# Six score banks filled by four row tiles at once, 256-query attention chunks, and an issue order that knows the array modes, in a two-layer attention and mixer kernel

## The chip, the cores and the metric

The kernel runs on one core of one Trainium2 chip. The metric is the device time of one execution in microseconds (us), taken on the slowest core, which here is the only one. The times of one kernel mostly agreed within 1% from run to run, so each number below is a median of several runs, and ratios have a 95% interval. For a program on one core the state of a single run cannot be told, but every profiled run of which several executions were timed was counted as fast. The span of a profiled execution is a little shorter than its device time. The kernel before was profiled in one more execution, of 591.3 us with a span of 589.2 us, which is not among the runs of its median.

The engines are named as in the profile: PE is TensorE (matrix multiply), PEld the weight loads of TensorE, DVE is VectorE, ACT is ScalarE, POOL is GpSimd and SP is the engine that issues the DMAs.

## The reference

The input `x` has 2048 tokens of 512 bf16 numbers. Two identical layers run on it. A layer is a causal attention with a sliding window of 256 tokens, 32 heads of 16 numbers each, and then an MLP that mixes over tokens.

```python
def _A_ref(x, wqkv, wo):
    B, S, D = x.shape                      # 1, 2048, 512
    H = 32; Dh = D // H; W = 256
    q, k, v = ...                          # x @ wqkv, cut into 32 heads of 16
    scores = jnp.einsum("bhqd,bhkd->bhqk", q, k) * (Dh ** -0.5)
    mask = (idx[:, None] - idx[None, :] >= 0) & (idx[:, None] - idx[None, :] < W)
    p = _softmax(jnp.where(mask[None, None], scores, -1e9))
    o = jnp.einsum("bhqk,bhkd->bhqd", p, v)
    return ...(o) @ wo

def _B_ref(x, w1, b1, w2, b2):             # w1: 2048 x 1792, w2: 1792 x 2048
    h = _layernorm(x, axis=-1)
    u = _gelu(jnp.einsum("bsd,sf->bdf", h, w1) + b1)
    y = jnp.einsum("bdf,fs->bds", u, w2) + b2
    return y.transpose(0, 2, 1)

x = x + _A_ref(_layernorm(x), wqkv, wo);  x = x + _B_ref(_layernorm(x), w1, b1, w2, b2)
x = x + _A_ref(_layernorm(x), wqkv, wo);  x = x + _B_ref(_layernorm(x), w1, b1, w2, b2)
```

## The kernel before

The kernel is written as a graph. Each operation says which engine it is for, what it reads and writes, a modelled cost and perhaps a priority. A list scheduler in the kernel's Python walks through the graph with the modelled costs and so fixes the order of instructions of every engine before the program runs. A `Pool` has a number of buffers; a `Tile` of a pool takes a buffer when its first operation is placed and gives it back after its last.

A head has only 16 numbers, so a head alone would use a small part of the 128x128 array of TensorE. The kernel takes the heads in four groups of eight ("octets", index `o`). Within an octet, two heads share a row tile of 32 partitions `r`. A score matmul reads 32 rows (`kbd`, keys of two heads in block diagonal form) and writes 128 partitions, so four of them, at the four row positions, can be in the array at once. The product of probabilities and values (PV, with `vbd`), and the sum of probabilities (the denominator, with `onesbd`), read 128 rows and write 32 partitions, so they use four column positions. All other matmuls use the whole array or halves of it. They are called fillers below: the projections to q, k and v, the output projection `wo`, the MLP.

PSUM has eight banks of 512 f32 columns. Before, they are given out as two score buffers of two banks (`psum2`), and four single banks (`psum`), of which fillers may hold two. A score operation computes two row tiles, over up to 512 columns, and ScalarE takes both in one exp instruction:

```python
psum2 = Pool("psum2", 2)
psum = Pool("psum", 4)
psum.classes = {"od": [0, 4], "f": [0, 2], "y": [0, 4]}
...
for u0 in range(0, len(lanes), 2):                    # two row tiles at a time
    ts = Tile(psum2)
    def f_sc(e, ts=ts, rr=prs[u0:u0 + 2], runs=runs, o=o):
        for j, q0, n, c0 in runs:
            tkk, jj = tk(j)
            for i, r in enumerate(rr):
                last = e.matmul(PS[:, 2 * ts.slot + i, c0 * 64:(c0 + n) * 64],
                                lhsT=kbd[32 * r:32 * r + 32, tkk.slot, o, jj, :, :]...,
                                rhs=qT[32 * r:32 * r + 32, tq.slot, o, q0 * 64:(q0 + n) * 64],
                                ..., tile_position=(32 * r, 0))
        return last
    prev_sc[0] = op("tensor", f_sc, ..., writes=[ts], prio=-1e6 + len(g.ops), ...)
    def f_exp(e, ...):
        return e.activation(pt[...], PS[:, 2 * ts.slot:2 * ts.slot + 2, 0:n], ACTF.Exp, scale=SMSCALE)
```

After a mask multiply on VectorE, PV and the denominator follow, in two separate banks `tO` and `tDen`, with 512 queries at a time. ScalarE computes one over the denominator as exp(-ln(d)), and VectorE multiplies. The scheduler picks by priority alone: scores, then PV, then fillers in program order. Fillers include a transpose of every token tile on TensorE, in `qkv`:

```python
def qkv(m):                                            # block m of 512 tokens
    for i in range(4):
        ft = filler()                                  # one of the two filler banks
        def f_tr(e, t=t, ft=ft):
            for c in range(4):
                last = e.transpose(PS[:, 4 + ft.slot, :]..., xh_sb[:, t, c * P:(c + 1) * P], ident[:])
        ...                                            # then a copy PSUM -> xhT on VectorE
...
for layer in range(2):
    prepare(0)                                         # layer 2: y of the first MLP, layernorm, qkv
    prepare(1)
    for m in range(4):
        tos[m] = attention(m, tqs[m], tks)             # 512 queries
        ...                                            # wo_block (4 tiles), prepare(m + 2)
    w1t = [load_w1(fb) for fb in range(7)]             # 1 MB each, two buffers w1b
    w2t = [load_w2(i) for i in range(8)]               # 0.9 MB each, two buffers w2b
    u_phase(w1t)                                       # u = gelu(w1^T h)
```

The second half of the MLP (`y_block`) of layer 1 is part of `prepare` in layer 2, so it runs as a filler between the scores of layer 2.

The softmax here doesn't subtract the row's maximum and nothing guards it: scores larger than these inputs give would overflow.

## Time and profile before

The time before was 593.02 us (three runs, 590.82 to 593.85). The span of the profiled execution is cut into five stages by the events on ScalarE: the first exp of layer 1, its last exp, the last gelu of layer 1, the first exp of layer 2 and its last exp.

| Stage | us | TensorE busy | ScalarE busy |
|---|---|---|---|
| start | 17.9 | | |
| attention of layer 1 (A1) | 172.3 | 155.8 | 155.6 |
| rest of the first MLP's u | 63.1 | 59.9 | 12.1 |
| gap without exp | 25.5 | 24.1 | 1.3 |
| attention of layer 2 (A2), with the rest of y of layer 1 | 194.2 | 180.1 | 156.7 |
| last MLP | 116.2 | 105.0 | 12.1 |

The table is read off the windows view of the kernel before, last five stages. Its columns are the window and its length in us, then busy us and, in brackets, the number of instructions of PE, PEld, DVE, ACT and POOL, then the granted TensorE clock as a share of full speed, the busy share of the DMA engines, and GB/s.

```profile
17.90:190.20 172.30, 155.77 (x2570) 73.17 (x2588) 118.00 (x245) 155.60 (x182) 68.80 (x109) 0.96 0.10 25
190.20:253.30 63.10, 59.91 (x290) 25.71 (x294) 7.73 (x18) 12.08 (x17) 3.04 (x8) 0.98 0.37 101
253.30:278.80 25.50, 24.07 (x166) 11.93 (x170) 18.03 (x37) 1.33 (x2) 10.31 (x22) 1.00 0.55 150
278.80:473.00 194.20, 180.11 (x2624) 80.19 (x2657) 125.57 (x245) 156.71 (x182) 61.45 (x99) 0.96 0.09 26
473.00:589.20 116.20, 105.04 (x486) 45.53 (x494) 18.91 (x34) 12.13 (x17) 3.04 (x8) 0.97 0.39 111
```

Two engines are 90% busy in A1, so neither alone is the limit at every moment. In A2 TensorE is 93% busy and ScalarE 81%. The next lines, from the page of the kernel before, are the busy sums of the engines, the granted TensorE clock in tenths for 40 equal slices of the span, and the groups of the exps and of the score matmuls. A group is line, engine, operation, output and inputs, shapes and count, then busy us and mean ns, then idle time of the engine ahead of them and what ended most of it.

```profile
PE 533.3 (91%) x6171; PEld 240.1 (41%) x6240; DVE 299.5 (51%) x610; ACT 339.1 (58%) x400; POOL 152.8 (26%) x266
PEclk9989999999995999999999999999999589999899
L600 ACT ACTIVATE pt<-PS 128x1024 bf16<-128x1024 f32 (+1 forms) x304 | 288.8, 1033 | 88.1 <-PE PS L587 71.4
L587 PE MATMUL PS<-qT,kbd 32*128 32x320 bf16 (+4 forms) x1440 | 120.9, 262 | 12.0 <-ACT pt L600 9.4
```

The exps cost 288.8 us in 304 instructions; ScalarE was idle 71.4 us in front of them because a score matmul had not been issued or was not done. The score matmuls kept TensorE busy for 120.9 us. The clock fell to half in two of the slices.

The next four lines, from the TensorE timeline of the kernel before (start us, busy us, instructions), show what a score operation costs between fillers.

```profile
104.17 0.39 PE L587 MATMUL PS<-qT,kbd 32*128 32x320 bf16 x4
104.49 0.60 PE L499 MATMUL PS<-xhT,wqkv 128*128 128x512 bf16 x2
105.03 0.39 PE L587 MATMUL PS<-qT,kbd 32*128 32x192 bf16 x4
105.36 0.60 PE L499 MATMUL PS<-xhT,wqkv 128*128 128x512 bf16 x2
```

Ends are modelled, so starts are what to compare. A score operation of 2 row tiles and 512 columns plus two full-array matmuls repeats every 0.86 us (104.17 to 105.03). Back to back, full-array matmuls of 512 columns follow each other every 0.216 us in most cases in this trace, so three passes of 512 columns (one for the score operation, two for the fillers) take 0.65 us. What remains, 0.21 us, is put down here to two changes of array mode, at about 0.11 us each. The Trainium skill says in "TensorEngine Tiling (Array Packing)", Key Properties, that "Changing tiling mode (not just tile) drains the TensorE", without a time.

The ScalarE timeline of the kernel before has one long hole in layer 2, and its chain of waits, in order of time (start us, us), goes through a weight load in each MLP.

```profile
379.49 2.85 ACT L600 ACTIVATE pt<-PS 128x1024 bf16<-128x1024 f32 x3 [20.53 <-PE PS L587]
```

```profile
207.99 6.07 DMA w1b<-in_B_w_dram
541.83 5.62 DMA w2b<-in_B_w_dram
```

The hole of 20.53 us ends with a score matmul: for that time TensorE worked on fillers, with no score operation ready to run.

### The profile page before, as it was taken

The page shows a single profiled execution, that of the slowest core. Times are in us where ns is not written, and L with a number is a line of the kernel's source. Part 1 is how long each engine was busy: PE and PEld are TensorE (multiplying, and loading weights), DVE is VectorE, ACT ScalarE, POOL GpSimd, SP SyncE. Part 2 cuts the span into 40 slices and gives each one's busy share as a digit, 9 for nine tenths or more (in the row PEclk, how much of TensorE's full clock was granted, in tenths as well). Part 3 has the DMA queues.
Part 4 walks back from the last instruction along what each step waited for, and adds up shares of the span by engine and source line. Part 5 has one row for each costly group of instructions (what it writes and reads, how often), then busy time and mean ns, then how long its engine had stood idle before and what let it go on. Part 6 is the DMA issues. An engine that isn't in the chain of part 4 may idle for free.

```text
span 589.2 us, 13839 instructions
## 1 busy us (share of the span) xinstructions
PE 533.3 (91%) x6171; PEld 240.1 (41%) x6240; DVE 299.5 (51%) x610; ACT 339.1 (58%) x400; POOL 152.8 (26%) x266
## 2 busy tenths in 40 slices
PE   4879999999988989989999999999998799997897
PEld 1435444444333434444344434434433343443343
DVE  5986665865873400056766466856687341001021
ACT  0678999699898121110998992299869821111000
POOL 3772433444320200015315212621453001000000
PEclk9989999999995999999999999999999589999899
DMA  8920000000000055572020022202000005251663
GB/s 276 225 54 3 3 1 2 3 2 2 1 2 2 1 143 142 143 197 63 2 63 3 2 59 69 63 3 61 5 2 3 1 1 142 71 143 28 186 187 117
DMA packets 68299, 36.55 MB, mean 62 GB/s; under 512 B 4752, under 2 KB 68240, under 8 KB 68240
## 3 DMA queue, kind: packets, MB, share of 16 engines
q1 hardware_dynamic: 68240, 35.66, 21.8%
q8 instruction: 49, 0.80, 0.6%
q14 instruction: 10, 0.08, 0.0%
HBM read 33.56 MB, written 2.10 MB: 61 GB/s over the span
## 4 chain that ended last, share of the span: by engine, by line
PE 57%; ACT 20%; DVE 14%; POOL 4%; DMA 3%; issue 2%; DVEq 0%; POOLq 0%
ACT pt L600 17%; PE PS L722 15%; PE PS L708 15%; PE PS L587 8%; PE PS L499 7%; PE PS L648 6%; DVE stats L438 4%; PE PS L524 4%; DVE x_sb L677 2%; POOL rstd L449 2%; PE PS L674 2%; DVE pt L621 2%; DVE xh_sb L451 2%; ACT rl L661 1%; ACT rl L663 1%
## 5 line engine op out<-in xcount | busy, mean ns | idle before, releaser
L600 ACT ACTIVATE pt<-PS 128x1024 bf16<-128x1024 f32 (+1 forms) x304 | 288.8, 1033 | 88.1 <-PE PS L587 71.4
L587 PE MATMUL PS<-qT,kbd 32*128 32x320 bf16 (+4 forms) x1440 | 120.9, 262 | 12.0 <-ACT pt L600 9.4
L722 PE MATMUL PS<-uT,w2b 128*128 128x512 bf16 x429 | 105.9, 385 | 10.8 <-DMA w2b<-in_B_w_dram 4.8
L708 PE MATMUL PS<-xh_sb,w1b 128*128 128x512 bf16 x436 | 101.0, 383 | 3.0 <-DVE xh_sb L451 1.0
L726 DVE SCALAR_TENSOR_TENSOR x_sb<-PS,b2col,x_sb 128x512 bf16<-128x512 f32 x32 | 22.9, 746 | 141.8 <-PE PS L722 141.8
L648 PE MATMUL PS<-pt,vbd 128*32 128x320 bf16 (+4 forms) x1440 | 86.4, 270 | 7.7 <-DVE pt L621 2.8
L621 DVE TENSOR_TENSOR pt<-pt,ldm 128x1024 bf16<-128x1024 bf16 (+2 forms) x104 | 65.8, 632 | 52.0 <-ACT pt L600 51.7
L648 PE MATMUL PS<-pt,onesbd 128*32 128x320 bf16 (+4 forms) x1440 | 82.7, 267 | 0.0
L587 PEld LDWEIGHTS PS<-qT,kbd 32*128 32x128 bf16 x1440 | 40.5, 94 | 99.6 <-ACT pt L600 58.1
L715 ACT ACTIVATE uT<-PS,b1col 128x512 bf16<-128x512 f32 x28 | 19.2, 687 | 98.2 <-PE PS L708 98.2
L499 PE MATMUL PS<-xhT,wqkv 128*128 128x512 bf16 x227 | 68.5, 393 | 6.1 <-issue 4.4
L447 POOL TENSOR_SCALAR rstd<-agg 128x1 f32<-128x1 f32 x64 | 16.1, 251 | 220.1 <-DVE agg L440 217.6
L708 PEld LDWEIGHTS PS<-xh_sb,w1b 128*128 128x128 bf16 x448 | 43.3, 98 | 56.8 <-issue 3.2
L510 POOL TENSOR_SCALAR kbd<-stg,par 128x512 bf16<-128x512 bf16 x64 | 50.1, 795 | 62.2 <-DVE stg L507 62.0
L722 PEld LDWEIGHTS PS<-uT,w2b 128*128 128x128 bf16 x448 | 39.4, 98 | 63.2 <-issue 9.4
L536 POOL TENSOR_SCALAR vbd<-stg,half 128x512 bf16<-128x512 bf16 x64 | 49.5, 784 | 48.8 <-DVE stg L533 45.4
L648 PEld LDWEIGHTS PS<-pt,vbd 128*32 128x32 bf16 x1440 | 36.6, 98 | 49.6 <-issue 18.6
L619 DVE TENSOR_TENSOR pt<-pt,ldm 128x512 bf16<-128x512 bf16 (+1 forms) x80 | 32.6, 411 | 22.9 <-ACT pt L600 22.2
L438 DVE BATCH_NORM_STATS2 stats<-x_sb 128x6 f32<-128x512 bf16 x64 | 41.8, 680 | 0.6 <-DMA x_sb<-in_A_x_dram 0.3
L648 PEld LDWEIGHTS PS<-pt,onesbd 128*32 128x32 bf16 x1440 | 38.4, 100 | 3.9
L524 PE MATMUL PS<-wqkv,xhT 128*64 128x256 bf16 x512 | 37.7, 278 | 2.1 <-DVE xhT L490 1.0
L451 DVE TENSOR_SCALAR xh_sb<-x_sb,agg,rstd 128x512 bf16<-128x512 bf16 x64 | 29.0, 456 | 17.7 <-POOL rstd L449 17.1
(36 smaller groups left out, 321.3 us busy)
## 6 DMA issues: line engine op xcount, KB each, us to landing
w1b<-in_B_w_dram SPq DMA_DIRECT2D x14, 1024.0 KB, 6.0
w2b<-in_B_w_dram SPq DMA_DIRECT2D x16, 896.0 KB, 5.6
out_dram<-x_sb SPq DMA_DIRECT2D x16, 128.0 KB, 5.0
wqkv<-in_A_wqkv_dram SPq DMA_DIRECT2D x3, 512.0 KB, 7.1
x_sb<-in_A_x_dram SPq DMA_DIRECT2D x3, 512.0 KB, 8.8
x_sb<-in_A_x_dram SPq DMA_DIRECT2D x2, 256.0 KB, 3.2
wo_sb<-in_A_wo_dram SPq DMA_DIRECT2D x1, 512.0 KB, 9.8
bst<-in_B_b_dram SPq DMA_DIRECT2D x1, 3.5 KB, 9.5
```

The source lines that it names most:

```text
L438: op("vector", lambda e: e.bn_stats(stats[:, t, :], x_sb[:, t, :]), reads=[f"x{t}"], writes=[f"st{t}"], cost=dve_cost(512))
L451: op("vector", lambda e: e.tensor_scalar(xh_sb[:, t, :], x_sb[:, t, :], agg[:, t, 0:1], rstd[:, t, :], op0=ALU.subtract, op1=ALU.mult), re ...
L499: mm_group(ft, 4, lambda e, c: e.matmul(PS[:, 4 + ft.slot, :], lhsT=wqkv[:, c, which * 512 + o * P:which * 512 + (o + 1) * P], rhs=xhT[:, ...
L510: op("gpsimd", lambda e, h=h: e.tensor_scalar(kbd[:, tk.slot, o, :, h, :], stg[:, ts.slot, :].rearrange("p (s n) -> p s n", n=64), par[:, ...
L524: last = e.matmul(PS[64 * hf:64 * hf + 64, 4 + ft.slot, sc * 256:(sc + 1) * 256], lhsT=xhT[:, tx.slot, c, tok:tok + 64], rhs=wqkv[:, c, 10 ...
L536: op("gpsimd", lambda e, h=h: e.tensor_scalar(vbd[:, tk.slot, 2 * sp:2 * sp + 2, :, 16 * h:16 * h + 16], stg[:, ts.slot, :].rearrange("p ( ...
L587: last = e.matmul(PS[:, 2 * ts.slot + i, c0 * 64:(c0 + n) * 64], lhsT=kbd[32 * r:32 * r + 32, tkk.slot, o, jj, :, :].rearrange("p h n -> p ...
L600: return e.activation(pt[:, tp.slot, la:lb + 1:lb - la, 0:n], PS[:, 2 * ts.slot:2 * ts.slot + 2, 0:n], ACTF.Exp, scale=SMSCALE)
L621: return e.tensor_tensor(v, v, msk.unsqueeze(1).unsqueeze(1).to_broadcast([P, lanes, n, w]), op=ALU.mult)
L648: last = e.matmul(PS[32 * r:32 * r + 32, 4 + dst.slot, q0 * 64:(q0 + n) * 64], lhsT=w, rhs=pt[:, tp.slot, ln, c0 * 64:(c0 + n) * 64], star ...
L708: last = e.matmul(PS[:, 2 * tu.slot + tt, :], lhsT=w1b[:, tw.slot, sc, tt * P:(tt + 1) * P], rhs=xh_sb[:, sc, :], start=(sc == 0), stop=(s ...
L722: mm_group(ft, NFT, lambda e, fc: e.matmul(PS[:, 4 + ft.slot, :], lhsT=w2b[:, tw.slot, fc, k * P:(k + 1) * P], rhs=uT[:, fc, :], start=(fc ...
```

## The change

The intent is to make TensorE do less for the same exps. Its parts are these.

1. All four row tiles of a score operation are issued at once, into four of six score banks. Two exps of two banks each follow, as before.
2. Output and denominator of PV share one bank (256 columns each), so queries come in eight chunks of 256 instead of four blocks of 512. Only two banks are left for output and fillers.
3. The scheduler's choice on TensorE takes the current array mode into account, and its model charges 95 ns for a change of mode.
4. Token tiles of blocks 1 to 3 are transposed by DMA, not by TensorE (24 of 32 tiles over both layers).
5. The second block is prepared inside the attention, `y` is held until the first four matmuls of the last `u` block are placed, the weight loads wait for the scores of chunk 5, and copies out of PSUM on VectorE get a higher priority.

The diff, cut to this core:

```diff
-        psum2 = Pool("psum2", 2)
-        psum = Pool("psum", 4)
-        psum.classes = {"od": [0, 4], "f": [0, 2], "y": [0, 4]}
+        psum2 = Pool("psum2", 3)
+        psum = Pool("psum", 2)
+        psum.classes = {"od": [0, 1], "f": [0, 2]}
...
+    SWITCH = 95.0
+    def _rank(self, o, now, ready):
+        if o.cls is None:
+            return (0, o.prio if o.prio is not None else o.idx, o.idx)
+        if o.cls == "sc":
+            k = 0
+        elif o.cls == "pv":
+            k = 1 if self.cfg in ("sc", "pv") or now - ready[o.idx] > 2500 else 3
+        else:
+            k = 2
+        return (k, o.prio, o.idx)
...
+                if not wide:
+                    op("sync", lambda e, i=i, t=t: e.dma_start_transpose(xhT[:, tx.slot, :, i * P:(i + 1) * P],
+                                                                         xh_sb[:, t, :]),
+                       reads=[f"xh{t}"], writes=[(tx, i)], dma=True, cost=900, prio=-1e5)
+                    continue
...
-                        for u0 in range(0, len(lanes), 2):
-                            ts = Tile(psum2)
+                    tp, tA, tB = Tile(p_pt), Tile(psum2), Tile(psum2)
+                    def f_sc(e, su=su, tt=(tA, tB)):
+                        for k, o, base in su:
+                            for j, q0, n, c0 in plan[k][0]:
+                                for r in range(4):
+                                    last = e.matmul(PS[:, 2 * tt[r // 2].slot + r % 2, ...],
+                                                    lhsT=kbd[32 * r:32 * r + 32, ...], rhs=qT[32 * r:32 * r + 32, ...],
+                                                    ..., tile_position=(32 * r, 0))
+                    for i, ts in enumerate((tA, tB)):
+                        op("scalar", ... ACTF.Exp, scale=SMSCALE), reads=[ts, "acttab"], ...)
...
-                tO, tDen = filler(1, "od"), filler(1, "od")
+                            od[o] = Tile(psum, 1, "od")
...
+                lambda a, b: [tw] + [f"uT{fc}" for fc in range(a, b)], after=[u_ops[-8]])      # y_block
...
-            prepare(0)
-            prepare(1)
-            for m in range(NC):
+            prepare(0, True)
+            for c in range(2 * NC):
+                tos[c] = attention(c, tqs, tks)
+                if c == 5:
+                    late = [prev_sc[0]]
+                if c % 2 == 0 and c // 2 + 1 < NC:
+                    prepare(c // 2 + 1, False)
+                wo_block(c, tos[c], c == 2 * NC - 1)
```

## The prediction

> **What bounds the kernel now.** Cut by windows, the 589.2 us span is: start 17.9; attention of layer 1 172.3 (ScalarE busy 155.6, TensorE 155.8); first MLP 63.2; a gap of 25.4 with no exp (last gelu to first exp of layer 2); attention of layer 2 about 195 (ScalarE 156.7, TensorE 181.9); then 116 of dense MLP. Exps cost 288.8 us over 304 instructions; back to back they come every 0.97 us. Layer 1 attention is therefore nearly ScalarE-bound. Layer 2 also carries the y matmuls and is TensorE-bound: one ScalarE wait there for a score matmul is 20.5 us.
>
> In the timeline a score op of 512 columns (two row tiles, so 2 x 0.213 us) plus a 0.43 us filler repeats every 0.86 us; streaming is 0.64, so about 0.11 us goes to each change of array mode. The Trainium skill, "TensorEngine Tiling (Array Packing)", Key Properties, says a mode change drains the array; the trace agrees with 0.11 us. The instruction order has 309 and 346 changes in the attention stages, i.e. 34 and 38 us (estimate).
>
> **What changes.** Score cells and exps stay the same (304 instructions).
> - Four row tiles at once: score streaming falls from 32 to 16 us per layer. The same page (Gotcha 1) says row tiles need different PSUM banks; six banks allow that.
> - Mode changes fall to 201 and 216: -12 and -14 us.
> - PE transposes (24 of 32 tiles) become DMA transposes: about -2.5 us TensorE and -5 us VectorE per layer, with extra latency per tile.
> - ScalarE: 64 Ln/Exp pairs of 256 columns for 32 of 512: +2 to 3 us per layer.
> - PSUM fillers have one or two banks, one beside an open output bank.
> - The last chunk is 256 queries, so two tiles rather than four pass through wo and layernorm before the MLP (about 1.95 us VectorE each).
> - y is held behind the last u block, which should avoid the 5.6 us w2 wait on the chain at 541.8.
>
> TensorE work per attention stage (estimate, streaming plus changes): layer 1 from about 152 to 123 us, layer 2 from 198 to 172, some 17 of it before the first exp. ScalarE stays near 160. So of some 55 us removed from TensorE, layer 1 can return little (it was ScalarE-bound), layer 2 about 12 to 17: its order still has one stretch of about 16 us of fillers with no score op, against 20.5 us idle before.
>
> **Sum.** start 17.9; attention 1 about 169 (-3); MLP 1 58 (-5); gap 23 (-2); attention 2 182 (-13); last MLP 107 (-9); end unchanged: span 557, time about 559 us. Range 540 to 580. Faster by over 2%: 0.90; within 2%: 0.08; slower: 0.02.
>
> **What would show each step.** Exp count 304 and their busy sum near 289; score matmul start-to-start halved; ScalarE 90% or more in both attention stages; largest ScalarE wait in layer 2 below 16 us; no w2 wait in the last stage; TensorE idle waiting for ScalarE in layer 1 up strongly.
>
> **What would make it wrong.** TensorE less busy may be granted a lower clock: in this trace it fell to 0.50 at 180 to 190 us where fillers ran out, with TensorE about 80% busy. Half clock over much of layer 1 would make TensorE the limit again (time near 580). DMA transposes much slower than 3 us, or queued behind weight loads on the same queue, would delay K and V of the next block. A single output bank could stall PV and then scores. Upside: if the layer 2 fillers fit between exps, attention 2 nears 165 us and the time 540.

## The result and the profile after

The changed kernel took 562.62 us (four runs, 560.68 to 566.20) against 593.43 us (four runs, 590.82 to 595.18). The ratio is 0.9491, with a 95% interval of 0.9432 to 0.9551: faster. Ratios here and below are the mean time of one kernel's fast runs over that of the other's of the same rounds, so they are not quite the ratio of the medians that are quoted.

The windows view of the kernel after, cut by the same events, with the same columns:

```profile
16.20:185.40 169.20, 129.76 (x3209) 72.68 (x3235) 127.20 (x279) 158.87 (x214) 70.26 (x114) 0.94 0.16 35
185.40:244.50 59.10, 53.60 (x288) 23.70 (x294) 5.00 (x11) 11.72 (x18) 1.48 (x4) 0.94 0.34 89
244.50:269.20 24.70, 24.36 (x164) 11.80 (x167) 15.37 (x30) 1.28 (x1) 10.20 (x20) 1.00 0.28 78
269.20:451.70 182.50, 152.10 (x3331) 80.66 (x3373) 132.05 (x283) 157.53 (x214) 63.28 (x105) 1.00 0.22 52
451.70:560.80 109.10, 99.22 (x474) 44.13 (x476) 17.01 (x27) 11.74 (x18) 1.48 (x4) 0.98 0.41 118
```

| Stage | before | predicted | after | after minus before |
|---|---|---|---|---|
| start | 17.9 | 17.9 | 16.2 | -1.7 |
| A1 | 172.3 | 169 | 169.2 | -3.1 |
| first MLP | 63.1 | 58 | 59.1 | -4.0 |
| gap | 25.5 | 23 | 24.7 | -0.8 |
| A2 | 194.2 | 182 | 182.5 | -11.7 |
| last MLP | 116.2 | 107 | 109.1 | -7.1 |
| span | 589.2 | 557 | 560.8 | -28.4 |

In A1 TensorE lost 26.0 us of busy time (155.77 to 129.76) and the stage lost 3.1 us. ScalarE was busy 158.87 of 169.20 us there, 94%. In A2 TensorE lost 28.0 us and the stage 11.7. The busy sums, the clock and the groups that answer to those of before, from the page of the kernel after:

```profile
PE 466.9 (83%) x7500; PEld 236.5 (42%) x7584; DVE 306.9 (55%) x659; ACT 342.4 (61%) x464; POOL 152.4 (27%) x266
PEclk9999999999967989999999999999999998999999
L621 ACT ACTIVATE pt<-PS 128x1024 bf16<-128x1024 f32 (+1 forms) x304 | 293.7, 1037 | 62.2 <-PE PS L607 62.1
L607 PE MATMUL PS<-qT,kbd 32*128 32x64 bf16 (+3 forms) x1920 | 62.1, 236 | 18.8 <-ACT pt L621 17.3
```

The exps did not change: 304 instructions, 293.7 us. The score matmuls fell from 120.9 to 62.1 us, so TensorE does them in half the time. What TensorE waits for at a score operation rose from 9.4 to 17.3 us, and it is an exp: the score banks are full and ScalarE has not yet emptied them. This is how a saving on one engine turns into a wait for the next one.

The next two fences are from the timelines of the kernel after: the longest hole before an exp of layer 2 on ScalarE, then a score operation and the PV behind it on TensorE.

```profile
364.29 3.77 ACT L621 ACTIVATE pt<-PS 128x1024 bf16<-128x1024 f32 x4 [14.46 <-PE PS L607]
```

```profile
101.83 0.40 PE L607 MATMUL PS<-qT,kbd 32*128 32x256 bf16 x8
102.20 0.27 PE L647 MATMUL PS<-pt,vbd 128*32 128x192 bf16 x4
```

The hole fell from 20.53 to 14.46 us and is still there. This score operation of 512 columns and four row tiles, with the mode change after it, takes 0.37 us from start to start. The shortest such steps in the trace are 0.33 us, about the 0.32 us (104.17 to 104.49) of a score operation with two row tiles before.

The order of TensorE's instructions in the built program gives the number of mode changes up to the last score operation of each layer. For layer 2 the count starts at the last `u` matmul, so it has some 10 changes that lie in the gap before the first exp:

```
before   309 + 346 = 655
after    201 + 216 = 417
```

Two waits of the kernel after had no counterpart of that size before. These are its chain of waits (start us, us), its waits for weights (engine, line, what it waited for: us in total, times, longest us), and two stretches around the first two pieces of the chain in the windows view.

```profile
200.31 6.03 DMA w1b<-in_B_w_dram
466.02 5.81 DMA w1b<-in_B_w_dram
532.14 6.91 DMA w2b<-in_B_w_dram
```

```profile
PEld PS L713 <- DMA w1b<-in_B_w_dram: 9.5, 2, 4.9
PE PS L713 <- DMA w1b<-in_B_w_dram: 8.5, 2, 4.4
```

```profile
200.00:206.40 6.40, 2.02 (x11) 0.71 (x9) 0.00 (x0) 2.20 (x4) 0.00 (x0) 0.89 0.83 212
466.00:472.00 6.00, 1.84 (x9) 0.72 (x8) 0.00 (x0) 2.06 (x3) 0.00 (x0) 0.94 0.85 224
```

TensorE stood still for 4.4 us (6.40 - 2.02) and 4.2 us (6.00 - 1.84) while one block of `w1` came in. After each of them the granted clock was half for a while (0.50 from 205.0 to 211.8 us and from 471.3 to 474.7 us). There are only two `w1` buffers, and each is given back when its `u` block is done. A `u` block sums over all tokens, so it needs the layernorm of the last tile. Until that last tile is ready neither buffer can come free, and the third load cannot start. The kernel before has the same two buffers and such a load in its chain at 207.99 us, but there TensorE was idle for only 3.2 us of the whole stage (63.10 - 59.91). `e2_mode_blind` below points to what made it longer.

### The profile page after: what moved, and what is told of

Same layout as the page of the kernel before. It is cut to its first block, busy times and chain, and to the rows that moved or that the text cites. A ratio compares the mean times of both kernels' runs of the same rounds, so it can differ in the third digit from the quotient of the medians.

```text
span 560.8 us, 16670 instructions
## 1 busy us (share of the span) xinstructions
PE 466.9 (83%) x7500; PEld 236.5 (42%) x7584; DVE 306.9 (55%) x659; ACT 342.4 (61%) x464; POOL 152.4 (27%) x266
## 4 chain that ended last, share of the span: by engine, by line
PE 49%; ACT 20%; DVE 18%; POOL 5%; DMA 4%; issue 3%; POOLq 0%
ACT pt L621 18%; PE PS L713 16%; PE PS L728 15%; PE PS L647 7%; PE PS L526 4%; DVE stats L455 3%; DVE pt L631 3%; PE PS L607 3%; DVE xh_sb L468 2%; DMA w1b<-in_B_w_dram 2%; DVE x_sb L681 2%; POOL rstd L466 2%; PE PS L551 2%; DVE stg L560 2%; PE PS L678 1%
## 5 line engine op out<-in xcount | busy, mean ns | idle before, releaser
L621 ACT ACTIVATE pt<-PS 128x1024 bf16<-128x1024 f32 (+1 forms) x304 | 293.7, 1037 | 62.2 <-PE PS L607 62.1
L647 PE MATMUL PS<-pt,vbd 128*32 128x64 bf16 (+3 forms) x1920 | 84.0, 240 | 19.6 <-DVE stg L560 5.3
L631 DVE TENSOR_TENSOR pt<-pt,ldm 128x512 bf16<-128x512 bf16 (+1 forms) x192 | 78.7, 413 | 34.8 <-ACT pt L621 33.4
L647 PE MATMUL PS<-pt,onesbd 128*32 128x64 bf16 (+3 forms) x1920 | 82.7, 238 | 0.8 <-issue 0.8
L607 PE MATMUL PS<-qT,kbd 32*128 32x64 bf16 (+3 forms) x1920 | 62.1, 236 | 18.8 <-ACT pt L621 17.3
L526 PE MATMUL PS<-xhT,wqkv 128*128 128x512 bf16 x227 | 61.5, 389 | 12.2 <-DVE stg L534 3.7
L647 PEld LDWEIGHTS PS<-pt,vbd 128*32 128x32 bf16 x1920 | 45.1, 98 | 53.1 <-DVE oT L669 11.0
L607 PEld LDWEIGHTS PS<-qT,kbd 32*128 32x128 bf16 x1920 | 28.2, 94 | 66.7 <-ACT pt L621 44.8
L647 PEld LDWEIGHTS PS<-pt,onesbd 128*32 128x32 bf16 x1920 | 46.5, 99 | 1.2 <-issue 0.9
L466 POOL TENSOR_TENSOR rstd<-rstd,mhalf 128x1 f32<-128x1 f32 x64 | 37.3, 585 | 4.0
L664 ACT ACTIVATE rl<-PS 128x256 f32<-128x256 f32 x64 | 25.7, 401 | 20.0 <-PE PS L647 19.8
```

The source lines that it names most:

```text
L466: op("gpsimd", lambda e: e.tensor_tensor(rstd[:, t, :], rstd[:, t, :], mhalf[:], op=ALU.pow), reads=[f"rs{t}", "mhalf"], writes=[f"rs{t}"] ...
L526: mm_group(ft, 4, lambda e, c: e.matmul(bank(ft), lhsT=wqkv[:, c, which * 512 + o * P:which * 512 + (o + 1) * P], rhs=xhT[:, tx.slot, c, : ...
L607: last = e.matmul(PS[:, 2 * tt[r // 2].slot + r % 2, base + c0 * 64:base + (c0 + n) * 64], lhsT=kbd[32 * r:32 * r + 32, tk.slot, o, jj, :, ...
L621: op("scalar", lambda e, ts=ts, tp=tp, i=i, cols=cols: e.activation(pt[:, tp.slot, 2 * i:2 * i + 2, 0:cols], PS[:, 2 * ts.slot:2 * ts.slot ...
L631: return e.tensor_tensor(v, v, msk.unsqueeze(1).to_broadcast([P, 4, w]), op=ALU.mult)
L647: last = e.matmul(bank(t)[32 * r:32 * r + 32, den * 256 + q0 * 64:den * 256 + (q0 + n) * 64], lhsT=onesbd[:] if den else vbd[:, tk.slot, j ...
```

## The experiments

All experiments below start from the kernel after, unless said otherwise. Each was compared with the kernel before on the same chip; the medians of the kernel before in those rounds were 592.0 to 593.6 us. To compare an experiment with the kernel after, its median is set against 562.6 us.

The theory was: A1 is bound by ScalarE, so what TensorE saves there comes back only in part; A2 is mixed; half of the saving is score streaming and half is fewer mode changes. The rivals were that the gain comes from the shorter tails (256 queries) or from the other edits (order, transposes), with row tiling adding little.

### e1_two_rows: the row tiles in pairs again

```diff
-                        for k, o, base in su:
+                        for k, o, base, r0 in [(k, o, base, r0) for r0 in (0, 2) for k, o, base in su]:
                             for j, q0, n, c0 in plan[k][0]:
-                                for r in range(4):
+                                for r in (r0, r0 + 1):
```

> One change to the changed kernel: a score op runs its row tiles as two pairs, one after the other, as the kernel before did; schedule, banks and mode changes stay. TensorE streams up to 16 us more per layer. My theory (layer 1 attention is ScalarE-bound with some 45 us of TensorE slack, layer 2 is partly TensorE-bound): attention 1 grows by at most 3 us, attention 2 by 5 to 10 us, time 570 to 575 us. Rival (the saved streaming is on the path in both layers, so the row tiles are the whole gain): 590 us or more.

It took 564.28 us, ratio 0.9522 (0.9499 to 0.9546). The busy time of the score matmuls rose from 62.1 to 66.0 us only, and the step from a score operation to the PV after it stayed 0.37 us. The group and a line pair from the TensorE timeline of `e1_two_rows`:

```profile
L607 PE MATMUL PS<-qT,kbd 32*128 32x64 bf16 (+3 forms) x1920 | 66.0, 238 | 17.8 <-ACT pt L621 16.6 <-DVE qT L531 0.8
102.51 0.40 PE L607 MATMUL PS<-qT,kbd 32*128 32x256 bf16 x8
102.88 0.27 PE L647 MATMUL PS<-pt,vbd 128*32 128x192 bf16 x4
```

So the edit did not undo the change. The second pair of row tiles does not wait for the first: it uses other rows and other banks, and it runs beside it. It even overtakes. The first score operation of `e1_two_rows` has runs of 256, 192 and 64 columns, and the program has all three of the first pair before any of the second. In the trace's records all four matmuls of 256 columns start within 0.023 us, and the first one of 192 columns 0.12 us after the start. The expectation rested on the assumption that issue order serialises pairs, and that assumption fell. The kernel before paid for pairs because the two pairs were separate operations, with fillers and mode changes between them. This run tells nothing about the worth of four rows at once. `e9_scores_twice` was made for that.

### e2_mode_blind: the order without knowledge of modes

```diff
-        if o.cls == "sc":
-            k = 0
-        elif o.cls == "pv":
-            k = 1 if self.cfg in ("sc", "pv") or now - ready[o.idx] > 2500 else 3
-        else:
-            k = 2
-        return (k, o.prio, o.idx)
+        return ({"sc": 0, "pv": 1}.get(o.cls, 2), o.prio, o.idx)
```

> The list scheduler no longer looks at the array mode when it picks the next TensorE op (scores, then PV, then fillers, as before). By the instruction order the mode changes rise only from 201 to 208 and from 216 to 223 in the two attention stages. My theory: 14 changes at 0.11 us are 1.5 us, so 562 to 565 us. Rival (the order-aware choice is what made the changes fall, and is a main source of the gain): 570 us or more.

The model still charges 95 ns for a change; only the choice is blind to the mode. It took 556.45 us, ratio 0.9397 (0.9374 to 0.9419): 6 us faster than the kernel after, so both expectations missed. Mode changes rose only from 417 to 431 (208 and 223). The fall from 655 to 417 is therefore nearly all due to the larger score operations, not to the order-aware choice. A2 became 3.5 us longer (186.0), but the first MLP fell from 59.1 to 53.0 us and the last from 109.1 to 105.7. The windows view shows the first MLP of `e2_mode_blind`:

```profile
186.10:239.20 53.10, 51.16 (x289) 23.15 (x294) 4.85 (x11) 11.75 (x19) 1.48 (x4) 1.00 0.37 99
```

TensorE is idle 1.9 us there (53.10 - 51.16), against 5.5 us in the kernel after (59.10 - 53.60), and its clock is full. The instruction order of the end of the attention stage says why. P stands for PV matmuls, U for matmuls of `u` and W for those of `wo`, with their number:

```
after          ... P24 U8 P40 U16 P24 U8 W4 U4 W4 U188
e2_mode_blind  ... P24 U8 P40 U4  P24 U8 W8 U204
```

The order-aware choice put 16 `u` matmuls ahead of the last PV, because its rule ranks a PV that has waited less than 2.5 us behind fillers while the array is in a filler's mode. Everything at the end hangs on that PV: the `wo` of the last tile, its layernorm, all `u` blocks, and with them the return of the `w1` buffer. That fits the waits of TensorE for `w1`, which fell from 8.5 us in all to 3.0 us. It is read from the order and the waits: the last PV alone was not moved in the kernel after.

### e3_pe_transpose: all transposes on TensorE again

```diff
-                if not wide:
+                if False:
```

> All transposes of the normalised input are back on TensorE with a VectorE copy, none by DMA. My theory: TensorE gets 2.5 us and some 9 mode changes (1 us) more per layer, VectorE 5 us; layer 1 hides it, layer 2 pays 2 to 4 us: 564 to 567 us. Rival (the 2.5 us from issue to landing of a DMA transpose delays K and V more than it saves): below 561 us.

It took 573.39 us, ratio 0.9673 (0.9645 to 0.9702), 10.8 us slower than the kernel after; 564 to 567 had been expected. The windows view of its two attention stages:

```profile
16.40:189.20 172.80, 133.12 (x3289) 75.76 (x3322) 130.18 (x291) 158.75 (x214) 69.72 (x114) 0.95 0.11 26
272.90:464.20 191.30, 157.48 (x3341) 83.58 (x3379) 134.63 (x295) 157.78 (x214) 62.22 (x105) 0.98 0.16 42
```

A1 grew by 3.6 us and A2 by 8.8 us (191.3 - 182.5), while TensorE's busy time grew by 3.4 and 5.4 us. In A2 the stage grew by more than the work. The Trainium skill gives 390 ns for a 128x128 transpose on TensorE and 1309 ns for one by DMA ("VectorE: DVE Perf Modes", The three transpose paths). In `e3` the transposes of 128x128 on TensorE mostly follow each other every 0.056 us within a group of four. In the kernel after, one DMA transpose of 128x512 took 2.5 us from issue to landing, as the page's list of DMA issues shows (output and input, count, median us):

```profile
xhT<-xh_sb SPq DMA_TRANSPOSE x24, 2.5
```

So the slower path by duration was the better one here, because it uses neither TensorE nor a filler bank nor a copy on VectorE. Which of the three counts was not shown; see `e12_before_transpose`.

### e4_shared_weights: one pool of four weight buffers

```diff
-        w1b = sb("w1b", [P, 2, NT, 256])
-        w2b = sb("w2b", [P, 2, NFT, 256])
+        w1b = sb("w1b", [P, 4, NT, 256])
+        w2b = w1b
-        p_w1, p_w2 = Pool("w1", 2), Pool("w2", 2)
+        p_w1 = p_w2 = Pool("w", 4)
```

> The two double buffers of the weights become one pool of four buffers. In the changed kernel's trace TensorE idles about 4.4 us for the third w1 block in each MLP (both buffers are held until the last layernormed tile is there) and about 1 us for a w2 block near the end. My theory: these waits go, 552 to 556 us. Rival (DMA is at its limit there, the wait only moves to a later block): 560 us or more.

It took 547.23 us, ratio 0.9249 (0.9214 to 0.9283), 15 us faster than the kernel after. The windows view of its two MLP stages:

```profile
184.00:234.40 50.40, 50.13 (x259) 22.57 (x258) 5.00 (x11) 11.73 (x18) 1.48 (x4) 1.00 0.43 118
442.10:544.70 102.60, 98.63 (x505) 44.63 (x513) 17.01 (x27) 11.71 (x18) 1.48 (x4) 1.00 0.44 123
```

The first MLP fell by 8.7 us and the last by 6.5 us, TensorE is idle for 0.3 us of the first, and the clock is 1.00 in both. The waits for `w1` and `w2` are gone from the list of waits, and no weight load is among the longest pieces of the chain. It uses 8 KB of SBUF per partition and buffer for `w1` and 7 KB for `w2`, so four buffers of the larger size need 2 KB per partition more. The gain is more than the 8.6 us that TensorE stood still in the two stretches above. One more part can be read from the clock (0.94 to 1.00 in the first MLP, 0.98 to 1.00 in the last), since the half clock after the two stalls is gone too: TensorE's busy time in the first MLP fell from 53.60 to 50.13 us for the same work.

### e5_reciprocal and e6_before_reciprocal: the reciprocal on VectorE

These were to make ScalarE cheaper without touching TensorE, in the kernel after (`e5`) and in the kernel before (`e6`). If ScalarE bounds the attention, the gain should be larger in the kernel after.

```diff
-  op("scalar", ... e.activation(rl[:, tr.slot, 0, :], bank(t)[:, 256:512], ACTF.Ln), ...)
-  op("scalar", ... e.activation(rl[:, tr.slot, 1, :], rl[:, tr.slot, 0, :], ACTF.Exp, scale=-1.0), ...)
+  op("vector", lambda e, t=t, tr=tr: e.reciprocal(rl[:, tr.slot, 1, :], bank(t)[:, 256:512]),
+     reads=[t], writes=[(tr, 1)], cost=dve_cost(256, psum=True), prio=-1e5)
```

(`e6` has the same edit with `PS[:, 4 + tDen.slot, :]` of 512 columns as input.)

> The reciprocal of the softmax denominator moves from ScalarE (a Ln and an Exp per output, 128 instructions of 256 columns, about 0.29 us each in a busy row, 18 us per layer) to one VectorE reciprocal per output straight from PSUM. My theory (layer 1 attention is ScalarE-bound): attention 1 falls from 169 us by 10 to 18 us; attention 2, where TensorE and its fillers limit the first half, falls by 4 to 10 us; time 536 to 550 us, if the VectorE reciprocal takes under 1 us. Rival (layer 1 is limited by the in-order handshake of scores, PV and the single output bank rather than by ScalarE's busy time): change under 6 us in all.

> The same move in the kernel before (32 outputs of 512 columns; ScalarE loses about 16 us per layer). My theory: there TensorE is nearly as busy as ScalarE in layer 1 (155.8 against 155.6 of 172 us) and limits layer 2, so it returns under 6 us: 587 to 593 us. Rival (ScalarE alone bounds layer 1 in both kernels): 10 us or more faster, below 583 us.

`e5` took 593.40 us, ratio 0.9993 (0.9925 to 1.0061), and `e6` took 721.41 us, ratio 1.2115 (1.2022 to 1.2208), with a mean clock of 0.837. Both are confounded. The condition that the reciprocal costs under 1 us was not met, as the group of `e5_reciprocal` shows:

```profile
L664 DVE RECIPROCAL rl<-PS 128x256 f32<-128x256 f32 x64 | 112.1, 1751 | 12.8 <-PE PS L647 12.2
```

It took 1.75 us for 256 columns in `e5`, and 3.36 us for 512 columns in `e6`: 6.6 to 6.8 ns per column, about twice the sum of the two ScalarE instructions (0.401 us for the Ln and 0.440 us for the Exp in the kernel after, the means of their groups). VectorE was busy 170 us of the 188 us of A1 in `e5`, against 127 of 169 us in the kernel after. Neither run says anything about whether ScalarE was the limit, so another load was chosen, `e8_scalar_load`.

### e7_mode_bench: the cost of a mode change by itself

Six sequences of matmuls of 512 columns with no dependence between them were put behind the last operation of the kernel after: 32 of one kind (F full array, S four row tiles, P four column tiles), or 16 pairs of two kinds. The output of the kernel is not changed by it.

```diff
+        for kind in ("F", "S", "P", "SF", "PF", "SP"):
+            bench(kind, 32 if len(kind) == 1 else 16)
```

> The changed kernel with a block of matmuls added after its last y matmul, TensorE alone, nothing to wait for: 32 filler matmuls of 512 columns, 32 score ops (four row tiles of 512 columns), 32 PV ops (four column tiles of 512 columns), then 16 alternations each of score and filler, PV and filler, score and PV. My theory: each kind alone streams at 0.214 to 0.22 us per op, and an alternating pair takes 0.43 plus two mode changes of about 0.11 us, so 0.62 to 0.68 us. Rival (row and column tiles of one array can follow each other without a drain, the 0.11 us in the kernel is semaphore time): an alternating pair takes 0.43 to 0.46 us.

It (613.33 us) gave these lines in the TensorE timeline; rows between are left out.

```profile
558.75 7.08 PE L773 MATMUL PS<-xhT,wqkv 128*128 128x512 bf16 x31 [0.85 <-DVE x_sb L732]
565.77 7.08 PE L777 MATMUL PS<-qT,kbd 32*128 32x512 bf16 x128
572.78 7.09 PE L783 MATMUL PS<-pt,vbd 128*32 128x512 bf16 x128
...
581.43 0.39 PE L773 MATMUL PS<-xhT,wqkv 128*128 128x512 bf16 x1
581.75 0.40 PE L777 MATMUL PS<-qT,kbd 32*128 32x512 bf16 x4
582.08 0.39 PE L773 MATMUL PS<-xhT,wqkv 128*128 128x512 bf16 x1
```

Thirty-two of one kind take 7.02, 7.01 and 7.03 us from the first start to the first start of the next kind (one full-array record is missing). Each of these times ends with one mode change. Within a kind, one operation follows the other every 0.216 us (6.70 us for 31 steps), for all three kinds. A pair of S and F repeats every 0.649 us over 15 pairs, one of P and F every 0.651 us, and one of S and P every 0.656 us. With 2 x 0.216 us of streaming, a mode change costs 0.108 to 0.112 us in each of the three pairs. The 0.11 us that the prediction read off the timeline is confirmed. The 238 changes fewer are then worth about 26 us of TensorE time (an estimate, 238 x 0.11), as the prediction had it; no run puts these changes back into the kernel, so what they are worth in device time is not shown. Four row tiles of 512 columns cost the same as one full matmul. In `e9` below, a second pass over the same rows adds about 0.22 us to a score operation, so four row tiles at once are about four times as fast as one after the other on the same rows.

### e8_scalar_load: more work for ScalarE

```diff
+                        op("scalar", lambda e: e.activation(scr[:], ident[:], ACTF.Exp), reads=["ident", "acttab"],
+                           cost=act_cost(P, psum=False), after=[ex], writes=["scr"])
```

One useless instruction of 128 columns follows each exp.

> The changed kernel with useless work added to ScalarE alone: after each of the 304 exps one activation of 128 SBUF columns that nobody reads. Estimate from the 0.29 us of a 256-column Ln or Exp in a busy row: about 0.2 us each, 30 us per layer. My theory (attention 1 is ScalarE-bound with some 10 us of ScalarE idle time, attention 2 has some 24): attention 1 grows by 18 to 30 us, attention 2 by 10 to 25 us, time 592 to 615 us. Rival (the in-order handshake on TensorE or the single output bank sets the pace): attention 1 grows by under 8 us, time below 580 us.

It took 598.10 us, ratio 1.0082 (1.0038 to 1.0126). The windows view of its two attention stages:

```profile
16.00:209.90 193.90, 147.25 (x3235) 76.40 (x3234) 128.32 (x280) 187.49 (x365) 69.97 (x114) 0.84 0.14 31
293.40:486.00 192.60, 166.01 (x3333) 81.39 (x3334) 135.81 (x283) 186.93 (x365) 61.68 (x105) 0.95 0.21 50
```

In A1 ScalarE got 28.6 us more to do and the stage became 24.7 us longer: A1 is bound by ScalarE. In A2 ScalarE got 29.4 us more and the stage became 10.1 us longer: there a third of the load comes through, and the rest falls into time in which ScalarE was idle. In A1 the clock fell to 0.84, and TensorE's busy time rose to 147 us with the same matmuls, without becoming the limit. A lower clock cost little here, in a stage that waits for ScalarE.

### e9_scores_twice: score streaming doubled

```diff
-                                for r in range(4):
+                                for r in (0, 1, 2, 3, 0, 1, 2, 3):
```

Each score matmul is issued twice, with the same result. The score streaming is then what it was before, with the order of the changed kernel. The shortest step from a 512-column score operation to the next mode rose from 0.33 to 0.55 us.

> Useless work added to TensorE alone, in place of the first experiment, which did not serialise the row tiles: each score matmul is issued twice into the same place, so a 512-column score op streams 0.43 us, what two row tiles at a time would take; same schedule, same mode changes. TensorE gets 16 us more per layer. My theory: attention 1 grows by at most 4 us, attention 2 by 5 to 10 us, time 568 to 577 us. Rival (score streaming is on the path in both layers): 30 us or more in all, 590 us or above.

It took 580.39 us, ratio 0.9781 (0.9735 to 0.9827), 17.8 us slower than the kernel after. The windows view of its two attention stages:

```profile
17.10:190.40 173.30, 146.09 (x4185) 87.08 (x4186) 127.91 (x279) 160.30 (x214) 69.72 (x114) 0.99 0.17 35
274.60:467.60 193.00, 174.65 (x4323) 97.40 (x4322) 132.10 (x284) 160.92 (x214) 62.18 (x105) 1.00 0.21 50
```

TensorE's busy time rose by 16.3 us in A1 and the stage by 4.1 us. In A2 it rose by 22.6 us and the stage by 10.5 us. In size this is the picture of the change itself turned round (26.0 us saved for 3.1 us, and 28.0 us saved for 11.7 us). In place it is not. In A2 the change took ScalarE's idle time from 37.4 to 24.9 us, and nearly all of that is two holes before an exp: 20.53 us, which became 14.46 us, and 5.16 us at 438.85 us, which is gone. `e9` leaves the long hole (14.67 us) and adds 7 us of idle time in short ones. So the halved streaming is worth about 18 us, but it is not what shortened the long hole. The rival that TensorE binds both stages would have given 590 us or more and falls. The time was a little above the 568 to 577 us that the theory gave; the other stages add about 2 us of the span that have no reason in the edit.

### e10_weights_tail: the last PV first, with shared weight buffers

On top of `e4_shared_weights`, PV of the last chunk keeps its rank whatever the mode.

```diff
+        elif o.cls == "pvl":
+            k = 1
...
-                           holds=[to], prio=len(g.ops), cfg="pv", cls="pv")
+                           holds=[to], prio=len(g.ops), cfg="pv", cls="pvl" if c == 7 else "pv")
```

> The four shared weight buffers (547.2 us), and in the last chunk of each layer PV goes ahead of fillers again, as in the mode-blind run: the order then puts 4 u matmuls instead of 16 ahead of the last PV, and the two wo groups side by side. My theory: the mode-blind run won in the MLP by this alone; wo and the last layernorms come 2 to 3 us earlier per layer: 541 to 545 us. Rival (the mode-blind run won through its weight loads, which the shared buffers already cover): 546 to 549 us.

It took 547.85 us, ratio 0.9241 (0.9200 to 0.9281): the same as `e4`. The instruction order is that of `e2` at the end, so the edit did what it should. Once the third weight load does not wait for a buffer, TensorE is busy 51.16 of the 51.30 us of the first MLP and an earlier PV has nothing left to save. That fits `e2` and `e4` having gained in good part from the same wait, reached from two sides; the two gains do not add. The expectation that an earlier PV alone saves 2 to 3 us per layer missed.

### e11_wo_late: `wo` behind the other fillers

On top of `e10`, `wo` of all chunks but the last goes behind every other filler, with five `oT` buffers. It aims at the hole of 14.46 us in layer 2, in which `y` and `wo` run before the projections that the next scores need.

```diff
-                    start=(o == 0), stop=(o == 3)), [(to, o) for o in range(4)] + ["wo"])
+                    start=(o == 0), stop=(o == 3)), [(to, o) for o in range(4)] + ["wo"],
+                    prio=fprio() if wide else fprio() + 1e6)
-        oT = sb("oT", [P, 3, 4, 256])
+        oT = sb("oT", [P, 5, 4, 256])
```

> The run before this one, and wo of all chunks but the last ranks behind y and the projections, with five output tiles instead of three to hold the results. My theory: attention 2 starves ScalarE for 13.6 us at about its middle because fillers for the third block of tokens come late on TensorE; with wo moved to the last third, where TensorE idles, the longest exp gap falls below 9 us and the time to 534 to 541 us. Rival (VectorE, which gets the residual adds and layernorms of those chunks late, then limits the last third): no faster than the run before this one.

It took 545.54 us, ratio 0.9199 (0.9162 to 0.9236). This is the fastest version found, 2.3 us below `e10`, but the interval of its ratio overlaps that of `e10`, so the two are not told apart by the totals. The longest hole before an exp in layer 2 fell from 13.59 us in `e10` to 7.75 us, as the ScalarE timeline of `e11_wo_late` shows:

```profile
387.48 1.02 ACT L623 ACTIVATE pt<-PS 128x1024 bf16<-128x1024 f32 x1 [7.75 <-PE PS L649]
```

A2 fell from 183.7 to 178.9 us, less than the 5.8 us by which the hole shrank and less than expected, because other holes grew: the second longest rose from 1.89 us to 3.42 us. The 534 to 541 us expected was missed. A stage in which TensorE is busy 156.5 of 178.9 us and ScalarE 158.2 us (by the windows view) is limited now by how the two mesh.

### e12_before_transpose: DMA transposes in the kernel before

```diff
+                if m:
+                    op("sync", lambda e, i=i, t=t: e.dma_start_transpose(xhT[:, tx.slot, :, i * P:(i + 1) * P],
+                                                                         xh_sb[:, t, :]),
+                       reads=[f"xh{t}"], writes=[(tx, i)], dma=True, cost=900, prio=-1e5)
+                    continue
```

> One part of the change done alone: the kernel before, with the 24 transposes after the first block of each layer moved to DMA. By the instruction order TensorE loses 2.5 us of transposes and 6 to 9 mode changes (under 1 us) per layer, VectorE 5 us. Undoing the same part in the changed kernel cost 11 us. My theory: the larger part of those 11 us is that each transpose holds one of the changed kernel's two filler banks until VectorE has copied it; the kernel before has four such banks, so alone the move returns 5 us or less: 588 to 593 us. Rival (it is the TensorE and VectorE work itself, which counts in both kernels): 8 to 12 us, 581 to 585 us.

It took 597.98 us, ratio 1.0084 (1.0024 to 1.0144). The windows view of its two attention stages:

```profile
17.60:191.80 174.20, 159.78 (x2541) 71.65 (x2542) 117.11 (x233) 156.42 (x182) 68.46 (x109) 0.92 0.18 34
280.70:480.00 199.30, 186.19 (x2609) 77.82 (x2609) 123.19 (x233) 156.65 (x182) 59.46 (x99) 0.94 0.12 31
```

The transposes that were worth 10.8 us in the kernel after made the kernel before slower, by some 5 us (the interval allows 1.4 to 8.5 us), against an expected gain. A1 grew by 1.9 us and A2 by 5.1 us, and the granted clock was lower there (0.92 and 0.94, against 0.96 and 0.96), with TensorE's busy time up by 4.0 and 6.1 us although it had 96 transposes less to do in all. In A2 ScalarE's idle time grew by as much as the stage, from 37.4 to 42.6 us: the longest holes are now 18.70 and 7.28 us, at other places than before. So the worth of the DMA transpose is not its own; it depends on the kernel around it. That the two filler banks make the difference (in the kernel after one of them may be all there is beside an open output bank) is argued from the pools and not shown. The expectation is also loose there: the kernel before has four single banks, but fillers may hold only two of them. Why the clock fell in the kernel before is open too.

## Why the prediction was right

The predicted 559 us met 562.6 us, and the predicted direction was right. The points, one by one:

- **A1 is bound by ScalarE: right.** The stage was predicted at 169 us and took 169.2. ScalarE was busy 94% of it. `e8` put 28.6 us on ScalarE and got 24.7 us; `e9` put 16.3 us on TensorE and got 4.1 us. Idle time of TensorE in the stage rose from 16.5 us (172.30 - 155.77) to 39.4 us (169.20 - 129.76), as the prediction had asked.
- **The sizes on TensorE: right in sum.** A mode change costs 0.108 to 0.112 us (`e7`), and 417 changes are left of 655. Score streaming halved (120.9 to 62.1 us busy). The stages lost 26.0 and 28.0 us of TensorE's busy time, where the prediction had about 29 and 26.
- **A2 gains 12 us of it, with one hole left: right.** The stage was predicted at 182 us and took 182.5, with a largest hole of 14.46 us, below the 16 us given. What shortened that hole is open: it is 13.9 to 14.7 us in `e2`, `e3` and `e9` alike, so none of the parts undone there did it.
- **ScalarE 90% or more busy in both stages: wrong for A2.** It was 86% (157.53 of 182.50). The hole of 14.46 us alone is 8% of the stage, so the step contradicted the prediction's own estimate of that hole.
- **"y is held behind the last u block, which should avoid the 5.6 us w2 wait": wrong as a forecast of the chain.** A `w2` piece of 6.91 us stands in the chain at 532.14 us. It costs TensorE little: it was busy 6.16 of 7.00 us around it, by the windows view. The effect of the hold alone was not measured: with these pools the scheduler gets stuck without it.
- **"MLP 1 58 (-5)": right in size by luck, with an unforeseen wait in it.** The stage took 59.1 us, but 53.0 us in `e2` and 50.4 us in `e4`, where the wait is shorter or gone. The forecast gain was too small and the unforeseen wait made up for it. The waits of 4.4 and 4.2 us for `w1` were not in the prediction; it looked at `w2`, the longest wait for weights of the profile before, and not at who gives back the `w1` buffers. `e4` shows what removing both waits is worth: 15 us.
- **Mode changes fall because of the order: only partly stated, and to be corrected.** The prediction counted the changes from the finished order and did not say which part of the change brings them down. `e2` shows that the larger score operations do nearly all of it (14 of 238 come back without the order-aware rank), and that the rank costs 6 us on balance.
- **Transposes: the work was sized right, its worth was not.** The prediction gave them 2.5 us of TensorE and 5 us of VectorE per layer. By the groups of `e3` and of the kernel after, the copies on VectorE fell by 9.9 us in all (13.1 to 3.2), as predicted. The busy sum of the transposes on TensorE fell by 9.6 us (13.3 to 3.7), but that sum has modelled ends in it. From start to start a transpose takes 0.056 us, which makes 5.4 us for 24 tiles of four (an estimate), as predicted. Undoing them cost 10.8 us (`e3`), 8.8 of it in A2, where the expectation gave 2 to 4 us. As a lone change they lose about 5 us in the kernel before (`e12`). The right amounts of work did not give these numbers.
- **The clock as a danger: mostly not met.** The mean clock of A1 was 0.94. It fell to 0.53 and 0.55 in two stretches (160 to 168 us and 176 to 185.4 us, by windows), which the slices above show as 6 and 7, and ScalarE was busy about 90% of them. The Trainium skill gives the clock two states, 2.4 GHz and half of that, and the half one comes after an idle window of about 3.4 us ("TensorE: Matmul & The Clock Gate", Part 1). The half is in the trace (0.50 from 157.2 to 167.5 us and from 174.3 to 184.5 us). The idle window is there in front of the half clock in the MLP (4.4 and 4.2 us), but not in A1, where TensorE was busy 7.43 of the 10.3 us and the longest idle time around was 1.41 us. Why the clock fell there is open. `e8` shows that even 0.84 over all of A1 leaves ScalarE the limit.

Where the gain came from can be stated in single undos, which need not add up: score streaming about 18 us (`e9`), DMA transposes about 11 us (`e3`), and the order-aware rank minus 6 us (`e2`). The remainder of the 31 us, some 8 us, belongs to chunks of 256 queries, fewer mode changes through larger operations, the `y` hold and the priorities, which were not separated. Three things stay open: why the transposes help one kernel and hurt the other, what shortened the long hole in layer 2, and what six score banks add over four. A version with four banks did not run, because the scheduler gets stuck with it. No run puts two row tiles into one bank, so that need, which the prediction takes from the skill, is not tested here either.

## What to carry to other kernels

Before costing a saving, decide for each stage which engine ends the waits, and then check it with a dummy load on one engine and doubled work on the other: here 16 us of TensorE work was worth 4 us in one attention stage and 10 us in the next. When a stage gets shorter, look at the buffers that the next stage needs before it can start, since a load that was hidden may become a wait, and a pool shared between two kinds of load may cure it for little memory (15 us here, where the two waits themselves showed 8.6). A scheduling rule that saves a cost everywhere, such as avoiding a 0.11 us mode change, should not apply to the last operation that everything after hangs on.

## What the Trainium skill lacked or had wrong

- "TensorEngine Tiling (Array Packing)", Key Properties, says that a change of tiling mode drains the array but gives no time. `e7` measured 0.108 to 0.112 us with 512-column matmuls, for each pair of full array, four row tiles and four column tiles.
- "TensorE: Matmul & The Clock Gate", Part 3 (Measured speedup vs the span model), gives 3.07 times for four row tiles of 512 columns. Issued back to back in `e7`, a group of four followed the other every 0.216 us, as full matmuls did, and in `e9` a second pass over the same rows added about 0.22 us: about four times. The page does not say whether its figure is for a lone group, which was not measured here.
- The same page, Part 3 (The mechanism), says of matmuls "strict FIFO, no reordering". In `e1`, a matmul of the second pair of row tiles starts 0.10 us ahead of one of the first pair that stands before it in the program (0.02 against 0.12 us after the first start), and the pairs run side by side (62.1 us of busy time for all four in turn, 66.0 us for the pairs).
- "VectorE: DVE Perf Modes" (First, the fixed hardware budget) says that Reciprocal runs an iterative divide with a repeat count of 8, but gives no duration. It took 1.75 us for 128x256 and 3.36 us for 128x512 f32 from PSUM (`e5`, `e6`), which made it dearer than Ln and Exp on ScalarE.
- "VectorE: DVE Perf Modes" (The three transpose paths) gives the durations of the paths for 128x128. It has no figure for a 128x512 tile from SBUF to SBUF (2.5 us from issue to landing here), and does not say that the slower path can win: 10.8 us for the kernel after, while the kernel before lost about 5 us by it.
